# Alibi sliding-window attention and a hardswish layer on one core: the first part rewritten as a plan of steps, with v loaded in runs and w_in in two halves

## The chip, the cores and the metric

The kernel runs on one core of a Trainium2 chip. The metric is the device time of one execution in microseconds; less is better. A core has five engines that run their own instruction queues in order: TensorE (PE in the profile, with its weight loads as PEld), VectorE (DVE), ScalarE (ACT), GpSimd (POOL) and SyncE (SP). DMAs are issued from the queues of SP, ACT and POOL and share 16 DMA engines.

## The reference

Attention over 8 batches of 8 heads, 576 tokens of 64 numbers, then a layer over the 4608 tokens:

```python
window = 128; scale = 1.0 / np.sqrt(D)
scores = scale * np.matmul(q, k.transpose(0, 1, 3, 2))
rel = pos[:, None] - pos[None, :]
bias = slopes[:, None, None] * (-np.abs(rel))[None, :, :]
mask = (rel >= 0) & (rel < window)
attn = softmax(np.where(mask, scores + bias[None], -1e9))      # exp, then divided by the row's sum
x = np.matmul(attn, v).transpose(0, 2, 1, 3).reshape(B * S, H * D)   # 4608 x 512
h = x @ w_in                                                   # 512 x 2048
out = (h * np.clip(h + 3.0, 0.0, 6.0) / 6.0) @ w_out           # 2048 x 512
```

## The kernel before

**Attention.** The work goes by pairs of heads: pair `g` is batch `g // 4`, heads `2 * (g % 4)` and the next, 32 pairs in all. A query tile of 128 tokens sees the key tile on its diagonal and the one before, so each pair has diagonal scores (`pd`) and off-diagonal ones (`po`). For a pair, q and k are loaded as float32, cast to bf16 (`pr`), transposed on PE and copied to `qTb` and `kTb`. In batch 0 each pair is loaded by itself (`load_run`, 288 KB each), cast (`prepare`) and transposed (`transposes`). In batches 1 to 3 two pairs go together (`load_double`, `prepare_double`, `double`, `wide_double`). Later batches are loaded by tokens, cast into `tbuf` on POOL and transposed by a DMA (`xbar`). v is loaded by tokens in five pieces (`load_tokens`, packets of 256 bytes) and cast to `vbuf`, which has a column of ones, so that the product with v gives the row's sum as well. Scores go through `Exp` on ACT. For pairs 0 to 3 bias and mask are added by table matmuls (`tables_diag`, `tables_off`); for pairs 4 to 7 the diagonal is masked on POOL by `affine_select` (`mask_diag`); from pair 8 on both parts are masked so, from the score tile `sce` that stays in its banks. `attend` or `values` multiply with v and divide; `back` transposes the result into `xT`, a ring of four batches, on PE for batches 0, 1 and pairs 10 and 11, else by a DMA from SP.

**The layer.** Nine tiles of 512 tokens. An up unit (`moe_up`, 16 for a tile) is four matmuls of 512 columns (`hps`, line 501), `Relu` on ACT and the product on DVE (lines 520 and 521) into `gbuf`. A down unit (`moe_down`, 16 for a tile) is four more into `ops` (line 551); after four of these a quarter of the tile's output is copied and stored. `w_in` is loaded by four DMAs from POOL's queue, 512 columns each (`load_w_in`), `w_out` by four (`load_w_out`); both cast to bf16 on the way. Exponentials of batch 0 lie in `w_out_sb` until they are used, those of batch 1 in `gbuf[1]`.

**The order.** The kernel turns the scheduler off (`tc.manual_schedule`): each engine runs its instructions in the order in which the program writes them. `first_batch` does the attention of batch 0 while q, k, v and the first quarter of `w_in` come in; the first up unit is split (`up_begin`). `second_batch` scores pairs 4 to 7 between up units, then does their products with v. `segment` runs over pairs 8 to 31, with up and down units between its steps in numbers given by `FILLS`. `fill(n)` takes the next n units from the list `units`, which `ORDER` lays out.

**PSUM.** Banks are shared by tag: `sc` (score tiles, 2 buffers of two banks), `h` (2 buffers), `av` and `o` (one each).

Of the kernel before, what the change touches and what calls it, by code (L numbers as in the profile page):

```python
# [10 lines left out]
FP32 = mybir.dt.float32  # L11
# [7 lines left out]
def kernel(  # L19
# [29 lines left out]
    NB_FULL = 2  # L49
    RING = 4 * S  # L50
# [5 lines left out]
    ident = perm.tile([128, 128], BF16)  # L56
    bias3 = perm.tile([128, 1], FP32)
# [22 lines left out]
    p4buf = [held.tile([128, 2, 128], BF16, name=f"p4buf{i}") for i in range(2)]  # L80
# [122 lines left out]

    def prepare(g, copies):
        for nm, copy in zip("qk", copies):
            pr = prs.tile([128, RT * D], BF16, tag=f"pr{nm}", name="pr",
                          padded_shape=[128, 2 * RT * D])
            copy(out=pr, in_=runs[nm][:, g % NP, :])
            st[g, nm] = pr

    def transposes(g, copies):
        b, hp = divmod(g, NP)
        for nm, dst, copy in (("q", qTb[b % 2], copies[0]), ("k", kTb[b % 2], copies[1])):
            src = st.pop((g, nm))
            tp = ps_h.tile([128, RT, RP], BF16, tag="h", name="tp", padded_shape=[128, 16, 64])
            for t in range(RT):
                for e in range(2):
                    r = slice(e * D, (e + 1) * D)
                    nc.tensor.transpose(tp[r, t, :], src[r, ts(t, D)], ident[r, r])
            copy(out=dst[:, hp, :, :].rearrange("p j c -> p (j c)")[:, 0:S].rearrange(  # L220
                "p (a t) -> p a t", t=RT), in_=tp.rearrange("p t a -> p a t"))
# [121 lines left out]
    def scores(g):  # L343
        if full(g):
            scores_diag(g)
            scores_off(g)
            return
# [36 lines left out]
    def exp_diag(g, e):  # L384
        h = 2 * (g % NP) + e
        pd = st[g, "pd"]
        if not full(g):
            nc.scalar.activation(out=pd[:, e, :, :], in_=st["sce"][e][:, :, 0, :],  # L388
                                 func=ACT.Exp, bias=bias_d[:, h:h + 1], scale=scale)
            mask_diag(g, e)  # L390
            return
        sc = st[g, "scd"]
        if diag_tabled(g):
            if e == 0:
                nc.scalar.activation(out=pd.rearrange("p e j c -> p e (j c)"), in_=sc,
                                     func=ACT.Exp, scale=scale)
            return
        nc.scalar.activation(out=pd[:, e, :, :].rearrange("p j c -> p (j c)"),
                             in_=sc[:, e, :], func=ACT.Exp,
                             bias=bias_d[:, h:h + 1], scale=scale)  # L400
        mask_diag(g, e)

    def mask_diag(g, e):
        pd = st[g, "pd"]
        nc.gpsimd.affine_select(out=pd[:, e, :, :], in_=pd[:, e, :, :],  # L405
                                pattern=[[0, 4], [1, 128]], channel_multiplier=-1, base=0,
                                compare_op=ALU.is_ge, fill=0.0)

    def exp_off(g, e):
        h = 2 * (g % NP) + e  # L410
        po, sc, p4 = st[g, "po"], st["sce"][e], p4buf[g % 2]
        nc.scalar.activation(out=po[:, e, :, :], in_=sc[:, :, 1, :], func=ACT.Exp,  # L412
                             bias=bias_o[:, h:h + 1], scale=scale)
        nc.gpsimd.affine_select(out=po[:, e, :, :], in_=po[:, e, :, :],  # L414
                                pattern=[[0, 4], [-1, 128]], channel_multiplier=1, base=-1,
                                compare_op=ALU.is_ge, fill=0.0)
# [250 lines left out]

    def second_batch():
        for g in range(NP, 2 * NP - 1):
            if g < NP + 2:  # L670
                wide_double(1, 1, "kq"[g - NP], V)
            scores_diag(g)
            exp_diag(g, 0)
            exp_diag(g, 1)
            fill(1 if g == NP + 2 else 2)
            scores_off(g)
            exp_off_full(g)
            fill(2 if g == NP + 2 else 1)
            if g == NP + 1:
                cast_tokens(1, "v")  # L680
        for i in range(4):
            load_w_out(i)
        g = 2 * NP - 1
        scores(g)
        exp_diag(g, 0)
        exp_diag(g, 1)
        prepare_double(2, 0, (P, P))
        nc.gpsimd.memset(ldbuf[2][:, 0:1], 0.0)
        load_tokens(2, "v")
        prepare_double(2, 1, (P, P))  # L690
        for dp in range(2):
            load_double(3, dp, "k", nc.sync)
        load_tokens(3, "q")
        exp_off_full(g)
        fill(1)
        attend(NP)
        fill(1)
        attend(NP + 1)
        fill(1)
        back(NP)  # L700
        attend(NP + 2)
        fill(1)
        back(NP + 1)
        double(2, 0, "k", 0, "av", A)
        attend(NP + 3)
        back(NP + 2)
        double(2, 0, "k", 1, "av", A)
        wide_double(2, 0, "q", A)
        up_begin(1, 0, 3)
        back(2 * NP - 1)  # L710
        up_begin(1, 1, 3)
        done[0] = 2 * NP
        fill(2)
        scores(2 * NP)
# [3 lines left out]
    def segment(lo, hi, fills):  # L718
        for g in range(lo, hi + 1):
# [3 lines left out]
            if lo < g < hi and g != 3 * NP + 1:  # L723
                scores(g)
# [14 lines left out]
            if g > lo:  # L739
                values(g - 1, (0, 1, 2))  # L740
# [72 lines left out]
```

## Time and profile before

| | |
|---|---|
| median of 3 runs | 321.67 us (321.26 to 322.14) |
| the profiled execution | 323.39 us, span 321.4 us |
| PE busy | 309.9 us, 96% of the span |
| ACT, DVE, POOL busy | 195.8, 173.6, 140.2 us |
| granted clock of PE | 1.00 |
| moved by DMA | 51.90 MB, 161 GB/s on average |
| chain that ended last | PE 84%, DMA 7%, SP's queue 3% |

The span is the time from the first to the last instruction of the program; the execution's own time is 2.0 us longer. The page cuts the span into 40 slices of 8 us and gives each engine's busy share in tenths.

### The profile page before, as it was taken

The numbers are of one execution on the slowest core, as the hardware profiler recorded it, in microseconds if no ns is written. First come the engines' busy times: TensorE is split into PE (matmuls) and PEld (weight loads), VectorE is DVE, ScalarE is ACT, GpSimd is POOL, SyncE is SP. The second block draws the span as 40 slices with busy tenths as digits, with TensorE's granted clock in tenths as the row PEclk, the third lists the DMA queues.
The fourth block names the chain that finished last, engine by engine and source line by source line (L and its number), as shares of the span: only waits on it lengthen the run. The fifth ranks groups of instructions, "written<-read, shape, count | busy, mean of one in ns | idle before, by whom it ended". The sixth has DMA issues, their size and how long they took to land.

```text
span 321.4 us, 7126 instructions
## 1 busy us (share of the span) xinstructions
PE 309.9 (96%) x2776; PEld 164.8 (51%) x2776; DVE 173.6 (54%) x338; ACT 195.8 (61%) x334; POOL 140.2 (44%) x249
## 2 busy tenths in 40 slices
PE   7879898999999999999999999999999999999996
PEld 6555455454554454444677654444444444444443
DVE  6757565664445555655565546554655455455510
ACT  4748876877777766766676667666764344244401
POOL 7455295586393866276645662763331000000000
PEclk9999999999999999999999999999999999999999
DMA  7999999999999999999999999942212200000112
GB/s 269 205 319 200 233 274 185 234 241 210 201 248 169 217 198 217 196 222 216 208 202 203 228 182 191 246 78 86 23 55 66 73 34 35 33 33 35 65 53 77
DMA packets 131425, 51.90 MB, mean 161 GB/s; under 512 B 118976, under 2 KB 123328, under 8 KB 131392
## 3 DMA queue, kind: packets, MB, share of 16 engines
q1 hardware_dynamic: 126160, 45.36, 66.4%
q0 software_dynamic: 4224, 4.19, 8.4%
q10 hardware_dynamic: 1008, 1.90, 1.6%
q8 instruction: 21, 0.34, 0.5%
q14 instruction: 12, 0.10, 0.1%
HBM read 36.70 MB, written 9.44 MB: 144 GB/s over the span
## 4 chain that ended last, share of the span: by engine, by line
PE 84%; DMA 7%; SPq 3%; POOL 2%; ACT 1%; issue 1%; DVE 1%; ACTq 0%; POOLq 0%
PE ops L551 38%; PE hps L501 36%; DMA ldbuf<-in_q_dram 3%; PE sce L364 3%; PE av L441 2%; DMA w_in_sb<-in_moe_w_in_dram 2%; SPq L112 2%; PE av L433 2%; DMA ldbuf<-in_k_dram 2%; SPq L98 1%; PE ops L532 1%; POOL w_out_sb L171 1%; PE tp L242 1%; POOL pr L227 1%; ACT r L520 0%
## 5 line engine op out<-in xcount | busy, mean ns | idle before, releaser
L521 DVE SCALAR_TENSOR_TENSOR gbuf<-r,hps 128x512 bf16<-128x512 f32 x144 | 98.8, 687 | 102.2 <-ACT r L520 100.9
L520 ACT ACTIVATE r<-hps,bias 128x512 f32<-128x512 f32 x144 | 98.9, 689 | 88.6 <-PE hps L501 88.3
L501 PE MATMUL hps<-xT,w_in_sb 128*128 128x512 bf16 (+1 forms) x640 | 144.9, 358 | 1.7 <-DMA w_in_sb<-in_moe_w_in_dram 1.5
L551 PE MATMUL ops<-w_out_sb,gbuf 128*128 128x512 bf16 x560 | 137.9, 380 | 0.0
L501 PEld LDWEIGHTS <-w_in_sb 128*128 128x128 bf16 x640 | 59.1, 98 | 56.7 <-DMA w_in_sb<-in_moe_w_in_dram 2.3
L551 PEld LDWEIGHTS <-gbuf 128*128 128x128 bf16 x560 | 51.8, 98 | 56.4
L414 POOL TENSOR_SCALAR_AFFINE_SELECT po<-po 128x512 bf16<-128x512 bf16 x48 | 30.2, 633 | 32.7 <-ACT po L412 32.5
L405 POOL TENSOR_SCALAR_AFFINE_SELECT pd<-pd 128x512 bf16<-128x512 bf16 x48 | 29.6, 631 | 31.6 <-ACT pd L388 31.6
L388 ACT ACTIVATE pd<-sce,bias_d 128x512 bf16<-128x512 f32 x48 | 31.6, 683 | 5.4 <-PE sce L372 5.4
L194 POOL CAST tbuf<-ldbuf 128x512 bf16<-128x512 f32 (+1 forms) x45 | 25.5, 611 | 18.6 <-DMA qTb<-tbuf 9.4
L560 DVE COPY osb<-ops 128x512 f32<-128x512 f32 x33 | 22.7, 688 | 20.0 <-PE ops L551 19.9
L412 ACT ACTIVATE po<-sce,bias_o 128x512 bf16<-128x512 f32 x48 | 32.9, 686 | 0.0
L452 DVE TENSOR_TENSOR avs<-av,rc 128x384 bf16<-128x384 f32 (+1 forms) x48 | 23.6, 491 | 1.6
L441 PEld LDWEIGHTS <-pd 128*128 128x128 bf16 x192 | 14.3, 97 | 8.3 <-POOL tbuf L194 0.5
L433 PE MATMUL av<-vbuf,po 128*128 128x65 bf16 x192 | 18.0, 193 | 0.0
L441 PE MATMUL av<-vbuf,pd 128*128 128x65 bf16 x192 | 17.3, 194 | 0.3 <-ACT kTb L244 0.3
L187 POOL CAST vbuf<-ldbuf 128x1024 bf16<-128x1024 f32 x14 | 14.2, 1041 | 5.4 <-DMA ldbuf<-in_v_dram 5.4
L433 PEld LDWEIGHTS <-po 128*128 128x128 bf16 x192 | 14.3, 98 | 2.9 <-DVE avs L452 0.5
L227 POOL CAST pr<-ldbuf 128x576 bf16<-128x576 f32 x20 | 12.8, 668 | 6.0 <-DMA ldbuf<-in_k_dram 3.8
L417 ACT ACTIVATE p4buf<-sce,bias_d 128x64 bf16<-128x64 f32 x48 | 15.4, 321 | 0.0
L364 PE MATMUL sce<-qTb,kTb 64*64 64x192 bf16 (+1 forms) x368 | 11.9, 246 | 0.0
L364 PEld LDWEIGHTS <-kTb 64*64 64x64 bf16 x368 | 7.1, 106 | 8.6 <-issue 8.5
(104 smaller groups left out, 207.8 us busy)
## 6 DMA issues: line engine op xcount, KB each, us to landing
out_dram<-osb SPq DMA_DIRECT2D x33, 256.0 KB, 2.4
ldbuf<-in_v_dram SPq DMA_DIRECT2D x32, 256.0 KB, 5.1
ldbuf<-in_q_dram SPq DMA_DIRECT2D x20, 256.0 KB, 4.8
ldbuf<-in_k_dram SPq DMA_DIRECT2D x16, 256.0 KB, 4.5
ldbuf<-in_q_dram SPq DMA_DIRECT2D x12, 288.0 KB, 7.5
ldbuf<-in_k_dram SPq DMA_DIRECT2D x12, 288.0 KB, 7.8
w_in_sb<-in_moe_w_in_dram POOLq DMA_DIRECT2D x4, 512.0 KB, 9.6
w_out_sb<-in_moe_w_out_dram POOLq DMA_DIRECT2D x4, 512.0 KB, 10.2
```

The source lines that it names most:

```text
L194: nc.gpsimd.tensor_copy(out=tbuf[:m, :, j, :], in_=s[:m, j, :, :].rearrange("p (i e) d -> p i (e d)", e=2))
L364: nc.tensor.matmul(sce[e][lo:lo + 64, j, :, :].rearrange("p s c -> p (s c)")[:, ds(lo, n)], lhsT=kT[r, j, lo:lo + 64], rhs=qT[r, ds(128 * ...
L388: nc.scalar.activation(out=pd[:, e, :, :], in_=st["sce"][e][:, :, 0, :], func=ACT.Exp, bias=bias_d[:, h:h + 1], scale=scale)
L405: nc.gpsimd.affine_select(out=pd[:, e, :, :], in_=pd[:, e, :, :], pattern=[[0, 4], [1, 128]], channel_multiplier=-1, base=0, compare_op=AL ...
L412: nc.scalar.activation(out=po[:, e, :, :], in_=sc[:, :, 1, :], func=ACT.Exp, bias=bias_o[:, h:h + 1], scale=scale)
L414: nc.gpsimd.affine_select(out=po[:, e, :, :], in_=po[:, e, :, :], pattern=[[0, 4], [-1, 128]], channel_multiplier=1, base=-1, compare_op=A ...
L433: nc.tensor.matmul(out_av, lhsT=po[:, e, qt % 4 if full(g) else qt - 1, :], rhs=vb[:, qt - 1, h, :], start=True, stop=False)
L441: nc.tensor.matmul(out_av, lhsT=d, rhs=vb[:, qt, h, :], start=(qt == 0), stop=True)
L501: nc.tensor.matmul(hps[:, lo:hi], lhsT=w_in_sb[:, ks, ts(ms, 128)], rhs=xT[:, ks, ds(src, hi - lo)], start=(ks == 0), stop=(ks == n_ks - 1))
L520: nc.scalar.activation(out=r6, in_=hps, func=ACT.Relu, bias=bias3[:, 0:1], scale=1.0 / 6.0)
L521: nc.vector.scalar_tensor_tensor(out=gts[nt][:, ms, :], in0=r6, scalar=1.0, in1=hps, op0=ALU.min, op1=ALU.mult)
L551: nc.tensor.matmul(ops[nt, sub], lhsT=gts[nt][:, ms, ts(sub, 128)], rhs=w_out_sb[:, ms, :], start=(ms == 0), stop=(ms == n_ms - 1))
```

## The change

The hand-written functions `first_batch` and `second_batch` and the first twelve turns of `segment` are replaced by a list of about 770 steps, `PLAN`, in the order in which they are written to the engines' queues; `run_plan` looks each up in `STEPS` and calls it. A line is a step, its arguments and mostly the engine (V, P, A for DVE, POOL, ACT) or the bank. `segment` starts at pair 20.

What is different in the pieces: batch 0's v comes in runs of four tokens for 512 tokens (`ldv`, two DMAs of four heads) and by tokens for the last 64 (`ldl`); it is cast (`cr`) into `tbuf`, and matmuls with a 0/1 matrix (`sel`, `vp`) put the tokens in order, from where they are copied to `vbuf` (`ve`). `w_in` comes in two DMAs of 1024 columns (`wp`). Batch 0's results are kept in a part of `gbuf[0]` (`avs0`), with its products split by query tile (`vf`, `vr`, `vl`). Pairs 8 and 9 use the score form of pairs 4 to 7 (`QF = 10`), and `p4buf` has four buffers.

Steps that the text names: `c0` cast, `t0` transpose and `e0` copy out of batch 0's q or k; `pd`, `dt`, `de` the same for double pairs; `td`, `to` tables; `sd`, `so`, `sq` scores; `xt`, `xd`, `xo`, `xf`, `x4` exponentials; `md`, `mf`, `m4` masks; `at`, `va` products with v; `na`, `nv`, `nf`, `nr`, `nl` divisions; `bf`, `br`, `bk` transposes back, `ef`, `er`, `ek` their copies, `bx` the same by DMA; `u`, `ur`, `um` an up unit's three parts; `d`, `dc`, `ds` down unit, copy, store; `ldd`, `ldt` loads of doubles and of tokens; `ct` and `vt` casts of tokens and of v; `wout` a load of w_out; `wu` warm-up matmuls; `mem` memsets.

```diff
+    NB_ROOM = 2
+    QF = 10
...
+    sel = perm.tile([128, 4 * 130], BF16)
...
-    p4buf = [held.tile([128, 2, 128], BF16, name=f"p4buf{i}") for i in range(2)]
+    p4buf = [held.tile([128, 2, 128], BF16, name=f"p4buf{i}") for i in range(4)]
...
+    def s_c0(g, nm, eng):
+        pr = prs.tile([128, RT * D], BF16, tag=f"pr{nm}", name="pr",
+                      padded_shape=[128, 2 * RT * D])
+        C[eng](out=pr, in_=runs[nm][:, g % NP, :])
+        st[g, nm] = pr
...
+    def s_ldv(b, h, n):
+        nc.sync.dma_start(out=vsource(b)[0][:, ds(h, n), :],
+                          in_=v[b, ds(h, n), 0:512, :].rearrange("h (p t) d -> p h (t d)", t=4))
...
+    def unshuffle(b, h, n, j0, banks):
+        for t in range(4):
+            for i, ps in enumerate(banks):
+                r = slice(32 * (j0 + i), 32 * (j0 + i) + 32)
+                nc.tensor.matmul(ps, lhsT=SEL[r, t, 0:128], rhs=vruns[r, t, ds(h, n), :],
+                                 start=(t == 0), stop=(t == 3))
...
+    def s_vp(b, j0, t1, t2):
+        banks = [psum(t, 512).rearrange("p (h d) -> p h d", h=H) for t in (t1, t2)]
...
+    def s_wp(i, k0, n):
+        nc.gpsimd.dma_start(out=w_in_sb[:, ds(k0, n), ts(i, 1024)],
+                            in_=moe_w_in[ds(k0 * 128, n * 128), ts(i, 1024)].rearrange(
+                                "(k p) f -> p k f", p=128))
...
+    def run_plan(text):
+        for line in text.split("\n"):
+            if line.strip():
+                name, *args = line.split()
+                STEPS[name](*(int(a) if a.isdigit() else a for a in args))
+
+    PLAN = """
+wu 20
+c0 2 k A
+ldl 0
+ldv 0 4 4
+c0 0 k V
+td 0
+ldv 0 0 4
+mem 3
+mem 4
+wu 7
+t0 2 k av
+c0 2 q V
+c0 0 q A
+ldd 1 1 k 0
+c0 3 k P
...
+sd 0
...
+vt 1 4
+xo 0
+t0 3 q o
+pd 1 0 k 0 P
...
+cr 0 4 4 V
+to 2
+mem 2
...
+xt 1
+vp 0 0 o av
+ldt 1 v 2
+wp 0 0 4
...
+pd 1 0 k 1 P
...
+wp 1 0 4
+ldd 1 1 q 0
+sd 5
...
+sd 4
+xd 4 1
+ef 3 256 256 V
+u 0 5 av
...
+u 0 12 av
...
+at 5
...
+md 7 1
+wout 0
...
+md 7 0
+wout 2
...
+pd 2 1 k 0 P
+pd 2 0 k 1 P
...
+sd 8
+so 8
+mem 5
...
+wout 1
+wout 3
+ldd 2 1 q 0
+pd 2 1 q 0 V
...
+ldt 3 q 1
+pd 2 1 q 1 V
+ldt 3 v 3
...
+d 0 0 0 o
+d 0 0 1 o
...
+d 0 0 3 o
...
+vt 2 0
...
+va 8 0 3
...
+u 3 12 h
+ur 3 12
+um 3 12
+"""
...
-        load_tokens(0, "v")
         constants()
         memsets()
-        memsets_later()
-        first_batch()
-        second_batch()
-        fill(2)
-        segment(2 * NP, G, lambda g: FILLS.get(g, (1, 1, 1, 2, 0, 1, 2)))
+        run_plan(PLAN)
+        done[0] = 20 - 1
+        segment(20, G, lambda g: FILLS.get(g, (1, 1, 1, 2, 0, 1, 2)))
         done[0] = G
         fill(len(units))
```

More of the change, by code (lines that the diff above doesn't have):

```diff
@@ L202 @@
     st = {}
[L204 to L221, printed above, removed]
+    avs0 = gbuf[0].rearrange("p m c -> p (m c)")[:, ds(11 * NT, NP * NQ * 128)].rearrange(
+        "p (g j e d) -> p g j e d", g=NP, j=NQ, e=2)
     def prepare_double(b, dp, copies, nms="kq", early=None):
@@ L398, in exp_diag @@
[L398 to L407, printed above, removed]
@@ L668, in second_batch @@
[L668 to L714, printed above, removed]
@@ new lines @@
+um 0 0
+dt 1 1 k 0 9 sc
+br h
+de 1 1 k 0 9 A
+mem 1
+gl 2 0 P
+um 0 1
+er A
+ldd 2 1 q 1
+dt 1 1 q 0 9 sc
+de 1 1 q 0 9 V
+ldt 1 v 0
+u 0 4 av
+ldt 1 v 1
+ur 0 4
+um 0 4
+u 0 6 h
+ur 0 6
+um 0 6
+to 4
+so 4
+xo 4
+sd 6
+xd 6 1
+u 0 12 av
+u 0 3 h
+ur 0 12
+ur 0 3
+um 0 12
+vt 1 0
+u 0 8 o
+ldd 2 0 k 0
+um 0 3
+ur 0 8
+ldt 1 v 3
+u 0 2 h
+ur 0 2
+um 0 2
+xd 6 0
+u 0 9 av
+sd 7
+ldd 2 0 q 1
+vt 1 2
+ldd 2 0 q 0
+xd 7 1
+ldd 2 0 k 1
+um 0 8
+xd 7 0
+u 0 11 h
+ur 0 11
+pd 2 0 q 0 A
+md 6 0
+ldt 2 v 4
@@ new lines @@
+um 1 7
+xf 9 1
+d 0 2 3 h
+dt 2 1 q 5 9 sc
+ldd 3 1 k 0
+va 8 0 3
+nv 8 0 3
+dc 0 2 A
+de 2 1 q 5 9 A
+u 1 8 h
+ct 3 q 2
+mf 9 1
+u 1 14 h
+xf 9 0
+ldt 4 q 2
+ldt 3 v 1
+va 8 3 2
+nv 8 3 2
+x4 9 0
+md 9 0
+m4 9
+md 9 1
+mf 9 0
+ur 1 8
+bx 8
+sq 10
+x4 10 1
+xd 10 1
+md 10 1
+d 0 1 0 o
+x4 10 0
+ldt 3 v 0
+va 9 0 3
+xf 10 0
+ldt 4 k 2
+xf 10 1
+ur 1 14
+m4 10
+um 1 8
+ct 3 q 3
+ct 3 q 4
+xb 3 q
+nv 9 0 3
+ds 0 0
+u 1 5 h
+ur 1 5
+d 0 1 1 o
+um 1 14
+va 9 3 2
+nv 9 3 2
+d 0 1 2 o
+xd 10 0
+u 1 9 h
@@ new lines @@
+x4 12 0
+ldt 4 q 3
+va 11 0 3
+d 1 0 1 h
+d 1 0 2 h
+nv 11 0 3
+d 1 0 3 h
+dt 3 1 k 0 5 h
+ldt 4 k 3
+ldt 4 k 0
+ct 4 q 0
+md 12 1
+m4 11
+ct 4 q 1
+ds 0 2
+d 0 3 1 o
+va 11 3 2
+ct 4 q 2
+dc 1 0 A
+ct 4 q 3
+nv 11 3 2
+ldt 3 v 4
+ldt 4 v 2
+sq 13
+d 0 3 2 o
+xd 13 1
+bk 11 av
+ldt 4 k 1
+ct 4 q 4
+xb 4 q
+ek 11 V
+ds 1 1
+de 3 1 k 0 5 V
+x4 13 0
+d 0 3 3 o
+u 2 1 h
+dc 0 3 V
+xf 13 0
+md 12 0
+xd 13 0
+mf 12 1
+mf 12 0
+u 2 11 h
+vt 3 0
+va 12 0 3
+ur 2 1
+um 2 1
+mf 13 0
+ur 2 11
+u 2 2 o
+ur 2 2
@@ new lines @@
+dt 3 1 k 5 9 h
+ldt 4 k 4
+nv 12 0 3
+vt 3 4
+x4 13 1
+u 2 0 av
+de 3 1 k 5 9 A
+um 2 11
+m4 13
+u 2 6 h
+um 2 2
+xf 13 1
+ur 2 0
+um 2 0
+u 2 13 o
+ur 2 13
+um 2 13
+u 2 3 h
+ur 2 6
+m4 12
+va 12 3 2
+sq 14
+x4 14 1
+ldt 4 v 4
+ldt 4 v 0
+xd 14 0
+ct 4 k 0
+ct 4 k 1
+u 2 12 o
+ur 2 12
+nv 12 3 2
+ct 4 k 2
+ct 4 k 3
+ct 4 k 4
+md 13 0
+ldt 5 q 2
+u 2 9 av
+um 2 6
+um 2 12
+x4 14 0
+ur 2 9
+d 1 2 0 h
+d 1 2 1 h
+um 2 9
+ds 0 1
+md 13 1
+mf 13 1
+va 13 0 3
+xf 14 1
+nv 13 0 3
+u 2 5 o
+xd 14 1
+xf 14 0
@@ new lines @@
+ur 2 3
+ur 2 5
+md 14 1
+um 2 3
+um 2 5
+va 13 3 2
+nv 13 3 2
+sq 15
+xf 15 0
+xf 15 1
+xd 15 0
+d 1 2 2 h
+u 2 10 h
+ur 2 10
+m4 14
+mf 14 0
+x4 15 0
+bx 12
+md 14 0
+xd 15 1
+mf 14 1
+va 14 0 3
+d 1 2 3 h
+dc 1 2 A
+u 2 7 o
+nv 14 0 3
+va 14 3 2
+mf 15 0
+u 2 4 h
+mf 15 1
+um 2 10
+md 15 0
+nv 14 3 2
+ur 2 7
+xb 4 k
+bx 13
+um 2 7
+md 15 1
+va 15 0 3
+nv 15 0 3
+x4 15 1
+m4 15
+d 1 3 0 h
+u 2 15 av
+ur 2 15
+um 2 15
+ldt 4 v 3
+sq 16
+ds 1 0
+xd 16 1
+ldt 5 q 1
+u 2 8 o
+ldt 4 v 1
+bx 14
+d 1 3 1 h
@@ new lines @@
+ldt 5 q 0
+ldt 5 q 4
+ur 2 4
+um 2 4
+vt 4 4
+ldt 5 q 3
+va 15 3 2
+nv 15 3 2
+bx 15
+ldt 5 k 0
+xd 16 0
+vt 4 2
+ds 0 3
+x4 16 1
+xf 16 0
+ur 2 8
+md 16 1
+md 16 0
+mf 16 0
+d 1 3 2 h
+d 1 3 3 h
+ds 1 2
+dc 1 3 A
+ds 1 3
+ldt 5 k 1
+x4 16 0
+vt 4 0
+ldt 5 k 2
+ldt 5 k 3
+m4 16
+ldt 5 k 4
+ct 5 q 0
+u 2 14 av
+ct 5 q 1
+ct 5 q 2
+ct 5 q 3
+ct 5 q 4
+ur 2 14
+xb 5 q
+d 2 0 0 h
+um 2 8
+d 2 0 1 h
+xf 16 1
+sq 17
+um 2 14
+mf 16 1
+d 2 0 2 h
+xd 17 0
+md 17 0
+d 2 0 3 h
+dc 2 0 V
+va 16 0 3
+ds 2 0
@@ new lines @@
+xd 17 1
+md 17 1
+nv 16 0 3
+u 3 0 h
+ur 3 0
+um 3 0
+xf 17 0
+mf 17 0
+x4 17 0
+u 3 1 h
+ur 3 1
+um 3 1
+d 2 1 0 o
+xf 17 1
+va 16 3 2
+mf 17 1
+x4 17 1
+m4 17
+nv 16 3 2
+bx 16
+u 3 2 h
+ur 3 2
+um 3 2
+ldt 5 v 0
+ldt 5 v 1
+ldt 5 v 2
+ldt 5 v 3
+ldt 5 v 4
+ct 5 k 0
+ct 5 k 1
+ct 5 k 2
+ct 5 k 3
+ct 5 k 4
+xb 5 k
+d 2 1 1 o
+u 3 3 h
+ur 3 3
+um 3 3
+sq 18
+d 2 1 2 o
+xd 18 0
+md 18 0
+u 3 4 h
+ur 3 4
+um 3 4
+xd 18 1
+md 18 1
+va 17 0 3
+nv 17 0 3
+d 2 1 3 o
+dc 2 1 V
+ds 2 1
+xf 18 0
+mf 18 0
@@ new lines @@
+x4 18 0
+u 3 5 h
+ur 3 5
+um 3 5
+u 3 6 h
+ur 3 6
+um 3 6
+xf 18 1
+mf 18 1
+x4 18 1
+m4 18
+va 17 3 2
+nv 17 3 2
+bx 17
+d 2 2 0 o
+ldt 6 q 0
+ldt 6 q 1
+ldt 6 q 2
+ldt 6 q 3
+ldt 6 q 4
+u 3 7 h
+ur 3 7
+um 3 7
+d 2 2 1 o
+sq 19
+u 3 8 h
+ur 3 8
+um 3 8
+xd 19 0
+md 19 0
+d 2 2 2 o
+xd 19 1
+md 19 1
+va 18 0 3
+nv 18 0 3
+u 3 9 h
+ur 3 9
+um 3 9
+xf 19 0
+mf 19 0
+x4 19 0
+d 2 2 3 o
+dc 2 2 V
+ds 2 2
+u 3 10 h
+ur 3 10
+um 3 10
+xf 19 1
+mf 19 1
+x4 19 1
+m4 19
+va 18 3 2
+nv 18 3 2
+bx 18
+u 3 11 h
@@ L757, in segment @@
                 scores(g + 1)
-            if g > lo and not by_xbar(g - 1):
+            if not by_xbar(g - 1):
                 back(g - 1)
```

737 lines of the change are left out of this document (638 added, 99 removed).

## The prediction

> **What bounds the kernel now.** I read the page first, then the windows by stage, the chain of waits in order of time, and the timeline of the first 30 us. The page:
>
> ```profile
> span 321.4 us, 7126 instructions
> ...
> PE 309.9 (96%) x2776; PEld 164.8 (51%) x2776; DVE 173.6 (54%) x338; ACT 195.8 (61%) x334; POOL 140.2 (44%) x249
> ...
> PE   7879898999999999999999999999999999999996
> ...
> DMA  7999999999999999999999999942212200000112
> ```
>
> PE fills the span, and the holes lie in the first seven slices of 8 us. The DMA engines are full up to 200 us. The windows split the holes by stage (columns: PE, PEld, DVE, ACT, POOL busy us; clock; DMA share, GB/s):
>
> ```profile
> 0.00:21.30 21.30, 17.00 (x357) 12.57 (x357) 15.08 (x49) 12.28 (x15) 11.83 (x30) 1.00 0.99 254
> 21.30:28.50 7.20, 6.11 (x56) 3.50 (x56) 3.92 (x7) 4.41 (x8) 4.27 (x7) 1.00 1.14 282
> 28.50:44.00 15.50, 14.38 (x147) 7.47 (x148) 8.68 (x12) 14.04 (x21) 8.11 (x13) 1.00 1.09 250
> 44.00:56.00 12.00, 10.84 (x134) 6.84 (x133) 8.13 (x15) 7.83 (x13) 8.65 (x15) 1.00 1.06 181
> 100.00:146.80 46.80, 46.80 (x414) 23.09 (x412) 27.66 (x55) 32.45 (x60) 28.12 (x51) 1.00 1.12 204
> ```
>
> Busy PE overstates it, since the end of each matmul is drawn late. So I use the starts in the trace: the gap from one matmul to the next counts as work up to what its width takes back to back (0.216 us for 512 columns, from "1.73 PE hps L501 x8"; 0.056 for 128), the rest as stall. That gives 294.9 us of work, 1.4 before the first matmul, 21.8 of stalls, and 3.1 from the last matmul to the end. Of the stalls 14.1 lie before 56 us, 4.8 from there to 146.8, 2.9 behind it. In the chain the early ones are transfers:
>
> ```profile
> 17.46 10.39 DMA ldbuf<-in_q_dram
> 28.52 7.26 DMA w_in_sb<-in_moe_w_in_dram
> 35.83 1.04 PE hps L501 x4
> ```
>
> **Where the change ends.** The plan replaces everything up to the scores of pair 20, and from there the loop is the old one. In the trace that point is 146.82 us (the 177th matmul of L364); 61 up units and 45 down units have started. Counting the plan's `u` and `d` lines gives 61 and 45 as well. So the result is one difference: when pair 20 starts. Before it PE has 126.7 us of work and 20.1 of waiting.
>
> **Work added on PE.** `vp` puts v's rows back in order with 16 matmuls of 512 columns on 32 rows each, two by two. Pairs on 64 rows start 3 ns apart in the trace, so one pair costs one matmul: 8 x 0.216 = 1.7 us; were they not side by side, 3.5. I take 1.7. Three warm-up matmuls less give back 0.2. Pairs 8 and 9 change their form of scores at about equal PE time (9 steps of 0.056 against about 0.4): 0.1.
>
> **DMA before the first up.** Packets of 2304 bytes take 93 ns when the queue is full, so a 288 KB load is 128 x 93 / 16 = 0.75 us. Batch 0's v is now 4608 packets of 256 bytes at 23 ns over 16 engines, 6.6 us. In runs it is 1024 of 1 KB and 512 of 256 bytes. No row has 1 KB on this queue; between 23 and 93 ns it is 2.2 to 6.7 us; by size 47 ns, so 3.7, saving 2.9. The eight weight loads of 512 KB come to 27 us of engine time, 3.3 each, so a half of w_in is 6.6.
>
> The rows that place them:
>
> ```profile
> 1.43 2.32 PE L153 MATMUL w<-ident 128*128 128x128 bf16 x20 [1.43 <-POOL ident masks.py:199]
> 4.74 0.72 PE L153 MATMUL w<-ident 128*128 128x128 bf16 x10
> 4.85 0.67 ACT L208 CAST pr<-ldbuf 128x576 bf16<-128x576 f32 x1 [0.65 <-DMA ldbuf<-in_k_dram]
> 6.88 0.40 PE L296 MATMUL scd<-qTb,kTb 64*128 64x128 bf16 x8 [0.73 <-ACT kTb L220]
> 12.41 0.88 POOL L166 DMA_DIRECT2D w_in_sb<-in_moe_w_in_dram  x1
> 21.34 0.90 PE L501 MATMUL hps<-xT,w_in_sb 128*128 128x512 bf16 x3 [0.20 <-DMA w_in_sb<-in_moe_w_in_dram]
> ```
>
> SP's queue after the runs (last packet 8.67): v0 until 12.4, then batch 1's k and q, with two small v pieces among them, until about 20.7. POOL issues `wp 0` behind `pd 1 0 k 0 P`, whose load lands at about 17.1 (0.7 from last packet to use, as the L208 casts show 0.5 to 0.9): cast 0.6, memset 0.45, issue at 18.1. First bytes come 1.6 later (12.41 to 14.00 before), so 6.6 us plus 1 of sharing end at 27.1, usable at 27.8. `wp 1` follows without a gap: 34.4.
>
> **PE up to the first up.** The plan casts pair 2 first on ACT, but its k arrives third (last packet 7.32), so ACT's first cast starts at 8.0, not 4.85, and pair 0's q cast is queued behind it: 9.3. With 18 transposes at 0.35, evacuations of 0.57 to 0.75 and casts of 0.52 to 0.67, pair 0 is scored at 11.5 instead of 6.88. The exponentials (1.02 each) then pace it with two score banks: pair 1 scored 16.8, `vp` 17.2 and 19.0, first values 20.8, norms of pair 3 by 25.9, `sd 5` 25.6, `sd 4` 27.6, first up at 27.9. Both ways give about 28, against 21.34 now. By then PE has done 16.2 us (sum of the plan's lines), 14.7 of which before also does; before had done that by 24.4. At its first up the new kernel is 3.5 us behind.
>
> **From there to 57 us.** To the scores of pair 8 the plan holds 25.3 us of PE work, 21.1 of ACT, 21.3 of DVE, 10.7 of POOL. `wp 1` is needed at 34.4 or a little later, exactly when it lands; the values of pair 5 need three v1 pieces, usable at about 39.4 and cast by 40.4, when PE is there. Followed by hand I lose 0.5. So pair 8 at 53.7, with work that before finishes at 55.5: now 1.8 ahead, because before stood at 28 and 35 for w_in (0.65, 0.97 us) and at 47.8 for a cast (1.16), and the plan has other work there.
>
> **w_out.** It goes out as 0, 2, 1, 3 between 43 and 49 (behind the masks of pairs 6 and 7 on POOL), 3.3 us each: 48, 51.3, 54.6 and 58, plus 0.7, plus what SP's q3 and v2 pieces take beside them: none to 5. PE wants part 1 at 57.9, part 3 at 61.6. Stall 0 to 3 us; taken 0.6. In before all four are issued at 43.55, and nothing waits.
>
> **The rest to pair 20.** Before stalls 4.4 us from 62 to 146.8. The plan's engine sums leave PE the fullest in each stretch (16.2, 18.5, 22.5, 23.2 us against ACT's 11.8, 13.5, 17.6, 15.9). At the pace of 100 to 146.8 us (1.6 in 46.8) the stalls would be 2.9; with one late transfer, 8. I take 4.4.
>
> **Sum:** 3.5 late, made good to 1.8 early, less 0.6: 1.2 us gained. The profiled execution took 323.39 us (span 321.4, 2.0 around it), so 322.2; it lies 1.7 above the median of the runs, so the median goes from 321.67 to about 320.5.
>
> **Rivals.** (a) The clock, to the slow side. After `wu 7`, at about 4.9 us, PE has nothing until pair 2's cast at 8.7: 3.8 us. Before never leaves it idle over 1.2 us. The first 20 warm-up matmuls ran at 0.107 us each, the later 10 at 0.056, so PE starts at half pace and needs about 2.8 us of dense work to leave it. If 3.8 us idle throws it back, the transposes and table matmuls behind 8.7 run at half pace until PE is dense again, which this head, 60% full, may not give before `vp`. Of about 8 us of work in that stretch half lies on the chain: 4 us; `wp 0` hides nothing of it, as both end at 28; some 1 us comes back at w_out: 3 - 1.2, so 323.5. The Trainium skill, TensorE: Matmul & The Clock Gate, Part 1, says that one idle window of about 3.4 us returns the clock to half; the 107 ns rows agree with its idle state, and no run here shows the return. The window runs freely, so 3.8 us need not hold a whole one. Chance 0.25.
>
> (b) The lead is kept: w_out lands in time, later stalls are 2.9. 1.8 + 1.5 = 3.3, so 318.4. For it: nothing but POOL's order holds w_out back. Against: DMA is full there. Chance 0.22.
>
> (c) SP's order, also slow: `ldt 3 v 3` waits for the last q cast of batch 2, at about 54, and v2, v3, q4 queue behind it. v2's last needed piece then lands at about 67.7, cast by 69.8, and PE wants it for pair 8 at about 71. Every us that cast is later costs one; 3 to 6 late gives 323 to 326. Chance 0.13.
>
> (d) The forecast, 320.5, chance 0.40: it spreads from 318.5 to 322.8 with the unknowns above.
>
> 0.3%, 1 us, is about what can be told from no change here. Faster by more: 0.21 of (d) and all of (b), 0.43. Slower: 0.04 of (d), 0.24 of (a), 0.12 of (c), 0.40. Same: 0.17. The range reaches from 317.0 (below (b), if both unknowns fall well) to 326.0 (the end of (c)).
>
> **What would show it.** Right: first `sd` at 11 to 12, first up at 27.5 to 29, `wp 1` landing at 34 to 35, pair 8's scores at 53 to 55, PE waiting for w_out by under 1 us, pair 20 at 145 to 146. Wrong: transposes behind 8.7 us at twice their 0.35; a first up after 30; waits on w_out or vbuf of over 2 us; pair 20 after 148.

## The result, and the profile after

The changed kernel takes 325.40 us (median of 4 runs, 324.22 to 326.44) beside 321.89 us (321.26 to 322.14) for the kernel before on the same chip: a ratio of 1.0111 [1.0062, 1.0160]. Slower by 1.1%, where 0.4% faster was forecast. The profiled execution took 326.44 us. Its page:

```profile
span 324.4 us, 7077 instructions
PE 309.6 (95%) x2746; PEld 167.3 (52%) x2785; DVE 178.1 (55%) x355; ACT 201.0 (62%) x344; POOL 130.7 (40%) x233
PE   4898989998999999999999999999999999999996
PEclk9599999999999999999999999999999999999999
DMA  7999699999999999999899999942111200000112
```

PE still fills the span and the holes are still in the first seven slices, the first of them deeper (4 for 7). New is the row of the clock: in the second slice, 8 to 16 us, PE was granted about half. (39 matmul records are missing, 2746 against 2785 weight loads; gaps of 0.2 us marked "issue" come from that and are not read here.)

The same windows as before (PE, PEld, DVE, ACT, POOL busy us; clock; DMA share, GB/s):

```profile
0.00:21.30 21.30, 16.04 (x263) 10.54 (x265) 11.52 (x42) 11.12 (x15) 9.51 (x23) 0.84 0.95 296
21.30:28.50 7.20, 6.44 (x126) 4.77 (x124) 5.36 (x14) 6.68 (x9) 2.58 (x4) 1.00 1.08 189
28.50:44.00 15.50, 14.10 (x140) 7.76 (x139) 9.93 (x19) 14.26 (x23) 4.56 (x9) 1.00 0.83 198
44.00:56.00 12.00, 11.81 (x160) 8.00 (x163) 11.30 (x21) 9.01 (x13) 9.02 (x15) 1.00 1.18 222
```

In the first one PE issues 263 matmuls instead of 357, at a clock of 0.84. In the third the DMA engines have room for the first time (0.83 for 1.09), in a window in which PE waits for a load of v, as the chain below shows.

The timeline, with the rows that answer to those of before (start, busy time, engine, line, in brackets the idle time before and what ended it; line 637 is `c0`, 646 `t0`, 279 `sd`, 900 `vp`, 919 `wp`, 459 the ups):

```profile
7.88 1.24 ACT L637 CAST pr<-ldbuf 128x576 bf16<-128x576 f32 x2 [3.55 <-DMA ldbuf<-in_k_dram]
8.60 1.57 PE L646 MATMUL bank<-ident,pr 64*64 64x64 bf16 x72 [3.26 <-ACT pr L637]
12.26 0.69 PE L646 MATMUL bank<-ident,pr 64*64 64x64 bf16 x18
12.88 0.61 PE L279 MATMUL scd<-qTb,kTb 64*128 64x128 bf16 x8
17.03 0.47 PE L646 MATMUL bank<-ident,pr 64*64 64x64 bf16 x18
19.25 1.04 PE L900 MATMUL bank<-tbuf,sel 32*128 32x512 bf16 x8
19.82 0.88 POOL L919 DMA_DIRECT2D w_in_sb<-in_moe_w_in_dram  x1
29.86 2.94 PE L459 MATMUL bank<-xT,w_in_sb 128*128 128x512 bf16 x11
```

PE stands for 3.26 us until ACT has cast pair 2's k. The same 18 transposes then show 0.69 us busy at 12.26 and 0.47 at 17.03. Pair 0 is scored at 12.88 (6.88 before), the first up starts at 29.86 (21.34 before). The trace's record of the clock is full from 6.04 us, half from 9.45 to 16.28, full from there: stretches of 3.41 and 6.83 us.

Behind the first up two more stalls stand in PE's list of waits (what waited, for whom: us in total, times, longest):

```profile
PE bank L646 <- ACT pr L637: 3.3, 1, 3.3
PE wide L399 <- POOL vbuf L672: 1.3, 1, 1.3
PE av L391 <- POOL po L932: 0.9, 1, 0.9
```

The chain of waits shows where the second comes from, and a chain step and a timeline row the third:

```profile
32.64 0.66 ACT pr L774
33.31 0.54 SPq L677
33.90 0.59 SPq L684
34.54 6.47 DMA ldbuf<-in_v_dram
41.14 1.04 POOL vbuf L672
42.88 1.05 POOL vbuf L672
```
```profile
60.36 0.67 DVE pr L774
61.05 0.37 SPq L684
```
```profile
72.40 2.03 POOL L672 CAST vbuf<-ldbuf 128x1024 bf16<-128x1024 f32 x2 [4.43 <-DMA ldbuf<-in_v_dram]
```

First: ACT casts a q of batch 1 at 32.64 and so frees a load buffer, for which SP's `ldd 2 1 q 1` has been waiting; behind it in SP's queue stand the loads of v1, which go out from 33.90 on, and PE stands from 42.7 to 43.98 for their cast. Then the same with batch 2: the cast of its last q at 60.36 lets SP issue `ldt 3 v 3` at 61.05, v2's pieces are behind that, and POOL casts v2 only at 72.40, after 4.43 us of waiting for it; its mask of `po` (line 932), on which PE waits until 75.07, is queued behind.

Pair 20 starts at 149.71 us against 146.82, so 2.89 later, and the span is 3.0 longer. All of the difference lies ahead of that point.

### The profile page after: what moved, and what is told of

Same layout as the page of the kernel before. It is cut to its first block, busy times and chain, and to the rows that moved or that the text cites. A ratio compares the mean times of both kernels' runs of the same rounds, so it can differ in the third digit from the quotient of the medians.

```text
span 324.4 us, 7077 instructions
## 1 busy us (share of the span) xinstructions
PE 309.6 (95%) x2746; PEld 167.3 (52%) x2785; DVE 178.1 (55%) x355; ACT 201.0 (62%) x344; POOL 130.7 (40%) x233
## 4 chain that ended last, share of the span: by engine, by line
PE 84%; DMA 6%; issue 3%; ACT 2%; POOL 2%; DVE 1%; SPq 0%; ACTq 0%; POOLq 0%
PE ops L509 24%; PE hps L459 22%; PE bank L459 11%; PE bank L818 10%; PE sce L347 3%; DMA ldbuf<-in_k_dram 2%; PE av L399 2%; DMA ldbuf<-in_v_dram 2%; PE av L391 2%; DMA ldbuf<-in_q_dram 1%; PE ops L490 1%; POOL vbuf L672 1%; PE sco L290 1%; PE bank L509 1%; ACT gbuf L658 1%
## 5 line engine op out<-in xcount | busy, mean ns | idle before, releaser
L478 ACT ACTIVATE r<-hps,bias 128x512 f32<-128x512 f32 x83 | 57.1, 688 | 64.5 <-PE hps L459 63.4
L479 DVE SCALAR_TENSOR_TENSOR gbuf<-r,hps 128x512 bf16<-128x512 f32 x83 | 57.0, 687 | 59.3 <-ACT r L478 58.4
L509 PE MATMUL ops<-w_out_sb,gbuf 128*128 128x512 bf16 x354 | 87.5, 379 | 1.5 <-issue 1.0
L459 PE MATMUL hps<-xT,w_in_sb 128*128 128x512 bf16 (+1 forms) x390 | 82.5, 344 | 0.2
L459 PE MATMUL bank<-xT,w_in_sb 128*128 128x512 bf16 x234 | 58.6, 379 | 0.7 <-issue 0.2
L811 DVE SCALAR_TENSOR_TENSOR gbuf<-r,bank 128x512 bf16<-128x512 f32 x61 | 41.1, 684 | 27.6 <-ACT r L806 27.1
L806 ACT ACTIVATE r<-bank,bias 128x512 f32<-128x512 f32 x61 | 41.3, 691 | 18.5 <-PE bank L459 17.4
L818 PE MATMUL bank<-w_out_sb,gbuf 128*128 128x512 bf16 x172 | 42.5, 379 | 0.8 <-issue 0.6
L658 ACT ACTIVATE pd<-sce,bias_d 128x512 bf16<-128x512 f32 x44 | 29.1, 686 | 6.4 <-PE sce L355 3.7
L518 DVE COPY osb<-ops 128x512 f32<-128x512 f32 x21 | 14.4, 687 | 17.3 <-PE ops L509 17.3
L966 POOL CAST tbuf<-ldbuf 128x512 bf16<-128x512 f32 (+1 forms) x25 | 14.5, 615 | 9.4 <-DMA qTb<-tbuf 5.0
```

The source lines that it names most:

```text
L459: nc.tensor.matmul(hps[:, lo:hi], lhsT=w_in_sb[:, ks, ts(ms, 128)], rhs=xT[:, ks, ds(src, hi - lo)], start=(ks == 0), stop=(ks == n_ks - 1))
L478: nc.scalar.activation(out=r6, in_=hps, func=ACT.Relu, bias=bias3[:, 0:1], scale=1.0 / 6.0)
L479: nc.vector.scalar_tensor_tensor(out=gts[nt][:, ms, :], in0=r6, scalar=1.0, in1=hps, op0=ALU.min, op1=ALU.mult)
L509: nc.tensor.matmul(ops[nt, sub], lhsT=gts[nt][:, ms, ts(sub, 128)], rhs=w_out_sb[:, ms, :], start=(ms == 0), stop=(ms == n_ms - 1))
L658: nc.scalar.activation(out=st[g, "pd"][:, e, :, :], in_=src, func=ACT.Exp, bias=bias_d[:, h:h + 1], scale=scale)
L806: nc.scalar.activation(out=r6, in_=st["u", nt, ms][0], func=ACT.Relu, bias=bias3[:, 0:1], scale=1.0 / 6.0)
```

## The experiments

Each kernel's ratio is to the kernel before, run in turn with it on the same chip. Executions of one kernel differ by 1 to 3 us, so verdicts go by ratios, and the profiles show the mechanism. Marks used: `sd 0`, first up, `sd 8`, pair 20 (start in us). `e0_control` is the changed kernel again.

> The changed kernel again, unchanged, beside the kernel before on the same chip. Its four runs lay near 324.3 and near 326.4. If the half clock in the head depends on where the clock's window falls, the clock records of this profile may differ from the first one's (half until 6.04, full to 9.45, half to 16.28 us), and the time with them. Expected 324 to 326.5, 3 to 4 us over before.

Measured: 1.0103 [1.0069, 1.0138]. `sd 0` 13.24, first up 29.70, `sd 8` 56.32, pair 20 149.93. The clock fell at 8.00 this time and came back at 14.82, again a stretch of 6.83 us. PE's stall for v1 is only 0.28 us, yet the three later marks agree within 0.3 us. The stall for `po` (0.92) is there again.

What v1 no longer costs, another load behind the same place in SP's queue does: batch 2's first q. ACT stands for it (1.49 us here, 1.41 in the first profile) ahead of its cast; an up unit's `Relu` is queued behind that cast, and the product and the divisions on DVE come after it. PE then waits 0.8 us in three places between 46 and 51 us, for DVE's divisions and for an exponential. So the v1 stall alone is not the price of the queue's order. ACT's timeline in `e0_control`:

```profile
44.73 0.67 ACT L774 CAST pr<-ldbuf 128x576 bf16<-128x576 f32 x1 [1.49 <-DMA ldbuf<-in_q_dram]
```

**The clock and the first cast.** Two ways to close PE's hole, and one to fill it:

```diff
-wu 7
+wu 60                 # e1_warm: 60 small warm-up matmuls
```
```diff
-        load_run(0, "k", nc.scalar)
-        load_run(0, "q", nc.sync)
-        load_run(1, "k", nc.scalar)
-        load_run(1, "q", nc.sync)
-        for g in (2, 3):
+        for g in (2, 0, 3, 1):     # e2_first
             load_run(g, "k", nc.scalar)
             load_run(g, "q", nc.sync)
```
```diff
-wu 7
+warm 15 av            # e4_warm2: 15 matmuls of 512 columns
```

> 60 warm-up matmuls in place of 7 ahead of pair 2's transposes, so that PE has work from 4.4 to about 8.5 us. Theory (the half clock from 9.45 to 16.28 us lengthens the chain of the head): no half clock after 6 us, pair 0's scores at about 12 instead of 12.88, the first up at about 28.7 instead of 29.86, and 1 to 1.5 us less in all. Rival (the head waits for casts, exponentials and w_in, and PE's pace is hidden): clock full, the first up within 0.4 us of 29.86, time as the control.

> The loads of batch 0's q and k are issued in the order 2, 0, 3, 1, in which the plan casts them. Theory (ACT's first cast waits for the third load until 7.88 us and everything in the head stands behind it): first cast at about 4.9, no idle stretch of 3.5 us on PE and no half clock after it, pair 0's scores at 9 to 10, the first up at 26.5 to 28, 2 to 3 us less than the control. Rival (w_in sets the first up): w_in's first half lands at about 28 as before, and the first up moves by under 1.5 us.

> 15 warm-up matmuls of 512 columns in place of 7 of 128, which fill PE to about 8.5 us with few instructions: the 60 small ones of e1 brought a fetch wait of 2.04 us at 12.7. Theory (half clock costs the head about 1.5 us): no such wait, full clock over the transposes of batch 0, pair 0's scores at 11.5 to 12, the first up about 1 us ahead of the control's 29.70, time 0.7 to 1.5 us less than the control's 325.5. Rival (the first up waits for w_in's first half, which lands at 28 to 29): the first up moves by under 0.5 us, time as the control.

`e1_warm`: 1.0174 [1.0125, 1.0223], slower; both theories missed. The clock was full from 5.59 on and `sd 0` came at 11.75. But PE then stopped in the middle of a row of 18 transposes, and the clock fell after all, at 15.83 for 3.41 us; the first up came at 31.46. The timeline:

```profile
14.72 0.28 PE L646 MATMUL bank<-ident,pr 64*64 64x64 bf16 x7 [2.04 <-issue]
```

"issue" means that no semaphore in the trace held it. That PE ran out of fetched instructions fits: 60 warm-up matmuls, each with its weight load, had run through in 4.1 us, and the DMA records hold a packet of 16 KB of the kind "instruction" from 12.25 to 13.33, where the stop (12.68 to 14.72) begins. But they do not say for which engine it was, so the cause is not shown.

`e2_first`: 1.0102 [1.0070, 1.0134], no gain; the rival had it. The first cast starts at 5.08 and `sd 0` at 11.63, but the clock is half all the same, from 8.54 to 15.36, and the first up waits 0.52 us for w_in. The window and the chain of `e2_first`:

```profile
9.00:16.00 7.00, 6.51 (x100) 3.84 (x101) 3.43 (x7) 4.21 (x6) 2.27 (x4) 0.55 1.11 315
```
```profile
19.88 9.35 DMA w_in_sb<-in_moe_w_in_dram
```

A PE that worked for only 1.8 of the 4 us behind 5 us lost the clock as an idle one does; and a head that is ready sooner meets a half of w_in that comes no sooner.

`e4_warm2`: 1.0049 [1.0030, 1.0068]; 0.54% or 1.7 us better than the control. Its timeline, and the window from 9 to 16 us of the changed kernel and of this one:

```profile
4.39 4.22 PE L631 MATMUL bank<-tab,ident 128*128 128x512 bf16 x15
8.82 1.33 PE L646 MATMUL bank<-ident,pr 64*64 64x64 bf16 x72 [0.22 <-ACT pr L637]
```
```profile
9.00:16.00 7.00, 6.43 (x146) 4.47 (x138) 3.79 (x6) 4.51 (x7) 3.10 (x4) 0.53 1.10 320
```
```profile
9.00:16.00 7.00, 6.00 (x189) 4.29 (x184) 4.73 (x9) 6.27 (x9) 3.10 (x4) 1.00 1.10 315
```

In the same 7 us 189 matmuls instead of 146, at full clock, and a busy time that is no longer. `sd 0` is at 11.89, and `sd 4`, just ahead of the first up, at 27.95 instead of 29.38. So the half clock has a price, some 1.7 us. Only 0.57 us of it is seen at the first up (29.13), which waits 0.79 us for w_in; the rest is seen at `sd 8` (54.45), where the stall for v1 is down to 0.2 and ACT no longer stands for batch 2's q. (The two ratios' uncertainties come to 0.4% together, so the price is known to about 1.3 us.)

**The loads of v.** In the plan, v1's three pieces move ahead of `ldd 2 1 q 1` (`gl 3 0 V` is a memset of one column that ties the buffer to DVE), then v2's four pieces ahead of `ldt 3 v 3` as well:

```diff
 ldd 1 1 q 0
+gl 3 0 V
+ldt 1 v 0
+ldt 1 v 1
+ldt 1 v 3            # e3_v1; taken out of their places among the ups
...
 ldt 3 q 1
+ldt 2 v 0
+ldt 2 v 1
+ldt 2 v 2
+ldt 2 v 3            # e6_v12 has both
```

> Three pieces of batch 1's v are loaded ahead of batch 2's first q load, behind a one-element memset on DVE at about 29 us, instead of behind that load at 34. Theory (the order of SP's queue makes pair 5's product with v wait 1.45 us at 42.5): that wait is gone, and the time falls by 1 to 1.5 us. Rival (the time is given back, because batch 2's loads and w_out come as late as before and later products wait for them): the wait is gone and the time falls by under 0.5 us; w_in's second half, which now shares the DMA engines, may land up to 2 us later and make the sixth up wait.

> e3 with batch 2's v loaded ahead of `ldt 3 v 3`, which waits on SP for the last q cast at 60.7. Theory (SP's order makes PE wait about 1 us for pair 8's masks at 73 to 75, because POOL sits before the cast of v): that wait is gone, pair 20 starts about 1 us ahead of e3's 147.94, time 324.65 to about 323.7. Rival (v2 now shares the DMA engines with w_out, which then comes late): PE waits for w_out at the second or fourth down unit by 1 us or more, no gain.

`e3_v1`: 1.0070 [1.0045, 1.0094], 0.33% better than the control; `sd 8` at 54.31, no stall for v1; the one for `po` remains (1.07 at 73.09). `e6_v12`: 1.0044 [1.0028, 1.0061], a further 0.26%; the stall for `po` is gone too and pair 20 starts at 146.50. So the two waits in SP's queue cost about 1 us and 0.8 us. Each of these is no larger than its uncertainty; both together, 0.59% off the control, are, and the lists of waits show each stall gone. The clock may have a part in these gains: with the control's head, full clock comes at 13.04 and 13.43 in these two profiles instead of 14.82, and `sd 5` at 26.80 in both instead of 27.36, before `e3_v1` issues its first moved load (28.39). How large that part is in the medians isn't shown: a run's mean clock does not tell it, which is 1.000 in `e3_v1`'s profile all the same.

**w_in sooner.** `e2_first` with the issue of w_in's first half moved up from behind `vp` to right behind `cr 0 0 4 P`:

```diff
 cr 0 0 4 P
+wp 0 0 4             # e5_win, with e2_first's order
```

> e2 (loads in the order of the casts) with the first half of w_in issued ahead of two casts on POOL that wait for batch 1's loads to 18.3 and 19.0 us. Theory (in e2 the first up waits for w_in, whose issue at 19.88 is behind these casts): issue at 15 to 16, landing at 25 to 26.5, no wait on w_in at the first up, first up at 28.5 to 28.8, since the chain of casts and exponentials then sets it; time 0.5 to 1 us less than e2's 325.7. Rival (batch 1's loads, now sharing with w_in, come later and the whole chain moves with them): first up at 29 or later and no gain.

Measured: 1.0134 [1.0113, 1.0154], no gain; the rival was right. (0.3% above `e2_first` is within the two uncertainties.) The transfer is issued at 16.00 instead of 19.88 and its first packet is 3.3 us earlier (18.2 for 21.5), but it lands only 1.0 us earlier, at 28.2 instead of 29.2, since it shares the DMA engines with batch 1's k and q. Those come late, as the list of waits says, and the first up is at 30.52:

```profile
PE wide L783 <- POOL pr L774: 1.7, 1, 1.7
```

`e7_all` put everything together, with two short rows of wide matmuls as fillers in the head:

```diff
+warm 4 h             # twice, ahead of t0 2 q o and of t0 3 k o
...                   # and the edits of e5_win and e6_v12
```

> e5 and e6 together, with 8 wide warm-up matmuls between the first transposes to hold the clock. If the three losses (late w_in and casts, half clock, SP's order) are separate and make up the difference to the kernel before: first up at 28 or earlier, pair 20 at 145.5 to 146.5, time 320.5 to 322, equal to before. If the new head costs more in itself (its work on PE and the single-buffered chain of exponentials): pair 20 at 147 or later and 323 or more.

Measured: 1.0058 [1.0027, 1.0089], a median of 324.22 us, which fits the second case (323 or more) and not the first. Its runs scatter (323.04 to 328.06), and the profiled execution is the longest of them, with the wait of `e5_win` again (2.33 us at 25.36), so its marks are not read. It tells nothing that `e5_win` and `e6_v12` do not.

**The three together, and what is left.** `e8_three` is `e4_warm2` and `e6_v12`:

> The three edits that each helped, together: wide warm-up matmuls (e4), batch 1's v ahead of batch 2's q (e3), batch 2's v ahead of batch 3's (e6). Theory (clock and the two places in SP's queue make up the whole loss, and add): ratio to the kernel before near 1.0107 - 0.0054 - 0.0033 - 0.0026, so 0.999 to 1.001; pair 20 at 145.5 to 146.5 in the profile. Rival (they overlap, since all delay the same chain): ratio 1.002 to 1.005 as e6 or e4 alone.

Measured: 1.0050 [1.0024, 1.0075], no better than either alone: the gains do not add. First up 28.60, `sd 8` 53.58, and there PE meets w_out. The timeline of `e8_three`:

```profile
58.98 1.89 PE L818 MATMUL bank<-w_out_sb,gbuf 128*128 128x512 bf16 x7 [0.99 <-DMA w_out_sb<-in_moe_w_out_dram]
```

Part 1 of w_out is the third that the plan issues, and it lands just ahead of that start, 11.6 us after its issue at 47.37. `e11_wout` issues 0, 1, 2, 3; `e12_wout_early` also puts 2 and 3 right behind 1, ahead of batch 2's loads:

```diff
 md 7 0
-wout 2
+wout 1
...
-wout 1
+wout 2
 wout 3               # e12_wout_early moves these two lines up to wout 1
```

> e8 with the loads of w_out issued in the order 0, 1, 2, 3 instead of 0, 2, 1, 3. In e8 the second down unit waits 0.99 us for part 1, the third load (last packet 57.14, PE goes on at 58.98). Theory (what the three edits win is handed back at w_out): that wait is gone, part 2 is in time at 58.6, the fourth down unit at about 61.7 may wait for part 3 (usable at about 63.4) by 0 to 1 us; pair 20 0.5 to 1 us earlier than e8's 146.93, ratio near 1.002. Rival (the remaining loss is not at w_out): the wait is gone and the ratio stays at 1.005.

> e11 with the last two loads of w_out also issued right behind the second, ahead of two casts and a memset on POOL (2 us). Theory: no wait on w_out at all, ratio 0.999 to 1.002. Rival (q3 and v2, which share the DMA engines, come later, or the two casts of batch 2's k hold the transposes ahead of pair 8): no wait on w_out, a new wait of 0.5 us or more between 48 and 75 us, ratio as e11.

`e11_wout`: 1.0031 [1.0011, 1.0051], the lowest ratio, still behind the kernel before; the wait for w_out is gone, pair 20 starts at 145.93. (The 0.19% to `e8_three` is within the two uncertainties.) `e12_wout_early`: 1.0054 [1.0027, 1.0081] with the same marks (145.96): nothing gained.

Is it the runs of v that cost? `e9_tokens` is `e8_three` with batch 0's v by tokens and without `sel`, `cr`, `vp` and `ve`:

```diff
-ldl 0
-ldv 0 4 4
+ldt 0 v 0            # to ldt 0 v 4
...
-ldv 0 0 4
...
-cr 0 0 4 P
+cv 0 0 P
...
-vp 0 0 o av
```

> e8 with batch 0's v loaded by tokens (4608 packets of 256 bytes) and cast straight to its place, so without the 16 matmuls that put runs in order. Theory (the first up waits for w_in, which waits behind all that the DMA engines moved before it): about 2.9 us more DMA work ahead of w_in, the first up 1.5 to 2.5 us later than e8's, time up by 1 to 2 us. Rival (PE's 1.7 us of added matmuls are what the runs cost): first up no later, time down by 1 to 1.7 us.

Measured: 1.0117 [1.0081, 1.0153], 0.67% or 2.2 us worse than `e8_three`; the theory, that transfers set the head, was right, though the wait is for a cast of batch 1 and not for w_in. PE's list of waits:

```profile
PE wide L783 <- POOL pr L774: 2.9, 1, 2.9
```

The 1.7 us of `vp` bring more than they cost, because batch 1's k and q come behind v on the same DMA engines: 2.86 us of waiting at 24.08, and a first up at 31.32.

Last, whether batch 1's second loads of q should make way for w_in: `e10_late` is `e8_three` with `ldd 1 1 q 0`, `q 1` and `ldt 1 v 2` held by memsets on DVE at 26.0 and 27.4 us:

```diff
+gl 0 1152 V
+ldd 1 1 q 0          # behind nl 3, with q 1; ldt 1 v 2 behind ef 1 0 512 A
```

> e8 with two q loads of batch 1 and one piece of its v (2.7 us of DMA work, not used before the first up) behind memsets on DVE at 27 to 28 us instead of ahead of w_in's first half. Theory (DMA work ahead of w_in sets the first up): w_in usable 1 us sooner, first up at 28.0 to 28.5 instead of about 29.1, since the chain of casts then sets it; time 0.5 to 0.8 us under e8. Rival (the work only moves behind, and the transposes of the second q double or pair 5's values wait for it): first up earlier, but a wait of 0.5 us or more between 30 and 45 us, and no gain.

Measured: 1.0240 [1.0206, 1.0274]; the rival by far. The first up is 0.4 us earlier (28.19), but DVE's cast of that q waits for its load, the product `um` of the first up is queued behind it, and PE waits for that. Its timeline:

```profile
33.21 0.75 DVE L774 CAST pr<-ldbuf 128x576 bf16<-128x576 f32 x1 [5.24 <-DMA ldbuf<-in_q_dram]
```

## Why the prediction was wrong

**Right.** The frame: the whole difference is when pair 20 starts (2.89 of 3.0 us). The cost of `vp`: its matmuls start two by two, some 0.22 us from pair to pair, so 1.7 in all. ACT's first cast at 7.88 (8.0 forecast). That the price of the runs is paid back in the DMA queues (`e9_tokens`).

**The head, 2.0 us.** The step that failed first is "pair 0 is scored at 11.5": 12.88, and 11.89 where the clock held (`e4_warm2`). Its transposes were costed at 0.35 us per 18, at full clock, and they ran at half: 0.62 us from the last row's start to the scores, 0.41 in `e4_warm2`. Rival (a), given 0.25, was what happened: 3.26 us of idle PE, and the half clock up to 16.28. The Trainium skill, TensorE: Matmul & The Clock Gate, Part 1, has the window run freely at some 3.4 us; the records here agree, in stretches of 3.41 and 6.83 us that began at 9.45, 8.00 and 8.54 in three executions. The prediction took that freedom as a reason for doubt; the two profiled executions of the changed kernel both show the half clock. As priced there (4 us) the rival was too dear; `e4_warm2` puts it at 1.7. With the clock held the chain comes nearly as forecast: `sd 5` at 25.93 and `sd 4` at 27.95 (25.6 and 27.6 in the prediction), where the changed kernel has 27.52 and 29.53.

The second step is w_in, "issue at 18.1" and "usable at 27.8". The prediction counts one cast on POOL ahead of the issue. The plan has another before that, `vt 1 4`: POOL waited 3.73 us for its load, the cast began at 17.94 and took 0.61, the next took 1.03 where 0.6 was put, and the issue came at 19.82. Batch 0's v isn't the reason: its last packet came at 12.59 (12.4 forecast), though packets of 1 KB took 59 ns on average in the DMA records, not 47. w_in landed at 28.1 in the changed kernel, ahead of PE; in `e4_warm2`, where PE is earlier, it landed at 29.1, and the first up stands for it until 29.13. So of 27.9 forecast and 29.86 found, mending the clock takes off 0.6 to 0.7, and w_in then holds the rest, 1.2.

(The "24.4" by which the kernel before has done the same work is 25.0 when counted again by starts; the sum goes on from pair 8, so nothing hangs on it.)

**From the first up to pair 8, 0.8 us.** Forecast 25.8, found 26.6. The loss is larger than 0.8, because a sum was wrong as well: "25.3 us of PE work" is 23.5 when counted by starts in `e6_v12` and `e12_wout_early`, whose profiles lack no matmul. So PE lost 3.1 us here where 0.5 was allowed; in `e6_v12` it loses 1.65. The step is "cast by 40.4, when PE is there": it took v1's loads as issued when the plan names them. They stood behind `ldd 2 1 q 1`, which waits for a buffer that ACT frees at 32.64, and POOL's two casts ended at 43.9; batch 2's q, behind them, held ACT (`e0_control`). The prediction followed POOL's queue and its own rule for SP's in one place only, for batch 2.

**w_out, 0.6 forecast, nothing found**, because PE came 2.8 us late. It was no error: with PE early the same stall is there, 0.99 us (`e8_three`).

**To pair 20, 1.3 us.** Forecast 91.9 from the scores of pair 8, found 93.25. Rival (c) had the mechanism and named the load, `ldt 3 v 3`; it happened later than priced, at 61.05, and cost less, 0.9 us of stall, because PE was late as well. "Every us that cast is later costs one" does not hold for a PE that is itself behind. The rest comes from the sum above: 88.7 us of PE work stand in this stretch by the same count, where the 91.9 is 86.6 of work, 4.7 of stalls and 0.6 for w_out. So 93.25 holds 4.55 us of stalls, less than the 5.3 allowed, the 0.9 among them.

**The addition.** The prediction gave a chance to one stall at a time. Three were there together, and the head's lateness hid parts of the others. Taken out singly they bring 0.54%, 0.33% and 0.26%; all three and the order of w_out bring 0.72% (1.0103 to 1.0031), not 1.13%. A better phase of the clock in `e3_v1` and `e6_v12` may also have counted part of the 0.54% twice.

**The base.** In the profiles `e11_wout` reaches pair 20 at 145.93, almost the forecast's 145.6, and 0.9 ahead of before; in the medians it is 0.3% behind. The profiled execution of before, 323.39, was above the median of every series of it (321.67 to 322.90); that of `e11_wout`, 322.83, is the fastest of its 11 runs, whose median is 323.68. So the sum was made against a long execution, with stalls that a median one need not have, and "so the median goes from 321.67 to about 320.5" let the change keep a gain of which about 1 us may have been that execution's alone.

**Open.** Where the last 0.3% of `e11_wout` lies: its profile has no stall over 0.25 us from 29 to 146 us, so what is left there is the head (first up at 28.74) and the 1.7 us of `vp`, which the DMA engines want; but that profile is its shortest execution, and the median one may have others. Whether w_in can come sooner without making batch 1 late was tried in two ways and failed in both; that there is none isn't shown.

## What to carry to other kernels

Before a price is put on a moved load, walk the queue that issues it up to the nearest instruction that waits for a buffer: the load goes out when that buffer is freed, whatever line it stands on. Where a reordered head leaves TensorE without work for some 3 us, cost what follows at half pace, or fill the hole with a few wide matmuls. When several stalls lie behind each other, mending one lends its time to the next, so single gains are not to be added, and a small gain is to be judged by ratios of many runs, never by two profiles.

## What the runs showed of the hardware

- The clock was lost with a PE that was not idle: with 1.8 us of matmuls in the 4 us ahead, the record shows half for 6.83 us (`e2_first`). 15 matmuls of 512 columns held it; 53 more small ones held it too, but were followed by a stop of 2.04 us with nothing to wait for (`e1_warm`). A wait of 2.86 us lost it again in `e9_tokens`: half from 23.78 to 27.19.
- The phase of the clock differs between executions of one program: in the changed kernel's two profiles it fell at 9.45 and 8.00, and with the same head `e3_v1` and `e6_v12` show no full clock at all before 13.04 and 13.43. The first up then lay at 29.86, 29.70, 29.15 and 29.15.
- Issuing a 1 MB transfer 3.9 us sooner brought its landing forward by 1.0 us (`e5_win` against `e2_first`), and batch 1's loads beside it came late: with full DMA engines (a share of 1.11 from 9 to 16 us in `e2_first`) a queue's order decides who comes late more than when the work is done.
- A load counts as landed only when the slowest of its 16 shares is through. In `e4_warm2`'s DMA records w_in's first half closes with 16 packets of 4 bytes, fifteen of them by 27.56 and the last at 28.75; it landed at 29.1. In the changed kernel the last came at 27.82, and it landed at 28.1.
